# Last four heads' keys gathered by DMA from spare rows, and masks and normalisations on VectorE or GpSimd

## The chip, the cores and the metric

The kernel runs on one core of a Trainium2 chip. The metric is the device time of one execution in microseconds (us); the time before is the median of 3 runs. One execution was also recorded by the profiler. TensorE appears in the profile as PE (its weight loads as PEld), VectorE as DVE, ScalarE as ACT, GpSimd as POOL, and the queue of SyncE, which issues all DMAs here, as SP.

## What is computed

A transformer block on 2,048 tokens of width 448, in bf16: attention over a dilated local window, then a gated mixer over all tokens.

```python
def _A_ref(x, wqkv, wo):              # H = 16 heads of Dh = 28, W = 8, dil = 2
    q, k, v = split((x @ wqkv).reshape(B, S, 3, H, Dh))
    idx = pos[:, None] - arange(8) * 2         # each token sees 8 earlier ones, 2 apart
    logits = einsum('bhsd,bhswd->bhsw', q, k[idx]) * Dh ** -0.5   # masked where idx < 0
    return einsum('bhsw,bhswd->bhsd', softmax(logits), v[idx]) @ wo

def _B_ref(x, w_in, w_sp, b_sp, w_out):        # F = 1792, Fh = 896
    z = gelu(x @ w_in)
    z1, z2 = z[..., :Fh], layernorm(z[..., Fh:])
    g = einsum('ts,bsf->btf', w_sp, z2) + b_sp
    return (z1 * g) @ w_out

h = x + _A_ref(layernorm(x), wqkv, wo)
out = h + _B_ref(layernorm(h), w_in, w_sp, b_sp, w_out)
```

## The kernel before, in words

**The order of the work.** The kernel is written as some hundreds of jobs: a name, an engine, what it reads and writes, and an estimated duration. `Planner.order` (L272) plays them through with a model of the engines and PSUM's eight banks; among the jobs that are ready it takes the one with the lowest number in `PRIO` (L27), a hand-tuned rank per job. `LOOK` (L25) says how long an engine may be held for a job that isn't ready yet, `SWITCH` (L20) what a change of matmul kind is charged on TensorE, and `ON` (L67) puts single jobs on another engine than their first choice. The outcome is one fixed list of instructions per engine. On the chip each engine works through its list in that order and waits at an instruction until its semaphores are there, so an estimate that is wrong shows as a wait. A job of kind F is a full matmul of 128 rows, H a pair of 64-row ones, L a logit job.

**Layer norm and transposes.** The 16 tiles of 128 tokens get their statistics on VectorE (L696, L698), the root on GpSimd (L690, L691), and the normalisation `n0_m` on VectorE (L707). The first four tiles are transposed on TensorE, the others by DMA, for which a small copy `nd` (L575) widens the tile first. The result is `xhT`. After attention the same is done for h (`n1`, into `hnT`).

**Queries and keys.** The tokens go in six stretches `QT` (L80), t = 0 to 5: two of 128 tokens, one of 256, three of 512. In each, four groups g of four heads are made (L776): the weights in `wqk` give one head 32 of the 128 output rows, of which the last 4 are zero padding (`wpad`, L763), since a head has 28 dimensions. A group is a product `qk{t}_{g}` of six full matmuls (q and k, three blocks of 128 input rows each) and one pair of 64-row ones (L564). Its two PSUM banks are then copied by one job `qe{t}_{g}` into `qkT` (L581), rows g of q at index 2g and of k at 2g+1; the last 128 tokens also go to `qkL`. The weights reach `wqk` from `wraw` in the copies `wp` (L575).

**Attention.** 17 blocks b of up to 128 queries. For each, two logit jobs `lg{b}_0` and `lg{b}_1` (L874), eight matmuls of 28 rows each. The first takes the heads in rows 0 to 63 of all four groups, the second those in rows 64 to 127. Two exponentials follow on ScalarE (L883), the mask `mk{b}` over 16 heads in one VectorE multiplication (L889), 16 matmuls with V (`o{b}`, L898), the reciprocal and the scaling on VectorE (L906, L909), a copy `od`, a transpose by DMA into `OTs` and a copy `oc` into `OT` (L581). `project` makes the output projection `y` and the residual (L843).

**The mixer.** z2 for each of the 16 tiles: product (L564), GELU, statistics (L969), `n2_m` (L978) on VectorE. Eleven of the 16 products may run before the last exponential; they are copied raw and get their GELU later. z1 in 14 units (L1010). Then g = w_sp z2 in 28 chains of 16 matmuls (L1043), bias and product on VectorE (L1051, L1054), and the output matmuls (L1066), written out by SP. The weights w_sp arrive by transposing DMAs (`wsp_la`, `wsp_lb`, `wsp_hi`).

## Time and profile before

| | |
|---|---|
| median of 3 runs | 243.05 us (242.62 to 243.81) |
| the profiled execution | 243.6 us, of which 241.9 us from the first to the last instruction (the span) |
| granted TensorE clock | 1.000 |
| instructions | 4,239 |
| HBM read, written | 6.83 MB, 1.84 MB |

A page of the profile gives, for each engine, its busy time and share of the span, the same in 40 slices (tenths), and the chain that ended last, followed backwards from the last instruction. Its groups read: line, engine, operation, output <- input, shapes, count | busy us, mean ns of one | idle time before it and what ended it. The timeline has: start, duration, engine, line, operation, and in brackets the idle time before it. Matmuls are pipelined and their ends are modelled, so the cost of a sequence is read from the starts or from the chain of waits.

### The profile page before, as it was taken

The page shows a single profiled execution, that of the slowest core. Times are in us where ns is not written, and L with a number is a line of the kernel's source. Part 1 is how long each engine was busy: PE and PEld are TensorE (multiplying, and loading weights), DVE is VectorE, ACT ScalarE, POOL GpSimd, SP SyncE. Part 2 cuts the span into 40 slices and gives each one's busy share as a digit, 9 for nine tenths or more (in the row PEclk, how much of TensorE's full clock was granted, in tenths as well). Part 3 has the DMA queues.
Part 4 walks back from the last instruction along what each step waited for, and adds up shares of the span by engine and source line. Part 5 has one row for each costly group of instructions (what it writes and reads, how often), then busy time and mean ns, then how long its engine had stood idle before and what let it go on. Part 6 is the DMA issues. An engine that isn't in the chain of part 4 may idle for free.

```text
span 241.9 us, 4239 instructions
## 1 busy us (share of the span) xinstructions
PE 235.4 (97%) x1707; PEld 115.5 (48%) x1726; DVE 155.0 (64%) x319; ACT 92.6 (38%) x115; POOL 55.4 (23%) x110
## 2 busy tenths in 40 slices
PE   7999999999999999999999999999999999999995
PEld 5674545545545444444344444444444444434443
DVE  6999878998999999998573135106111920805554
ACT  2779777778989765666230000000000000033000
POOL 8535116255565533061111000000000000000000
PEclk9999999999999999999999999999999999999999
DMA  6954497958533999999899400000000020010112
GB/s 194 317 138 94 77 157 176 171 133 190 109 62 72 176 152 179 228 158 153 166 204 178 42 0 0 0 3 0 0 0 3 0 76 0 20 41 0 57 38 76
DMA packets 65923, 23.21 MB, mean 96 GB/s; under 512 B 58352, under 2 KB 65648, under 8 KB 65904
## 3 DMA queue, kind: packets, MB, share of 16 engines
q1 hardware_dynamic: 65904, 22.95, 46.9%
q8 instruction: 13, 0.21, 0.4%
q14 instruction: 6, 0.05, 0.1%
HBM read 6.83 MB, written 1.84 MB: 36 GB/s over the span
## 4 chain that ended last, share of the span: by engine, by line
PE 92%; DMA 2%; DVE 2%; SPq 1%; issue 1%; ACT 0%; ACTq 0%
PE psum L1043 40%; PE psum L564 37%; PE psum L1066 9%; PE psum L874 3%; PE psum L898 3%; DMA wraw<-in_A_wqkv_dram 2%; DVE E L889 1%; SPq L605 1%; DVE qkT L581 1%; ACT wqk L575 0%; PE psum L738 0%; DVE srg L1073 0%; PE psum L740 0%; ACTq L179 0%
## 5 line engine op out<-in xcount | busy, mean ns | idle before, releaser
L1051 DVE TENSOR_TENSOR ub<-psum,bb 128x512 bf16<-128x512 f32 x28 | 19.4, 691 | 50.4 <-PE psum L1043 50.0
L1043 PE MATMUL psum<-wsp_hi,z2p 128*128 128x512 bf16 x217 | 50.6, 379 | 0.4
L1010 ACT ACTIVATE z1p<-psum 128x1024 bf16<-128x1024 f32 x14 | 14.1, 1021 | 95.8 <-PE psum L564 95.8
L1043 PEld LDWEIGHTS psum<-wsp_hi,z2p 128*128 128x128 bf16 x224 | 21.8, 98 | 26.2 <-issue 0.4
L883 ACT ACTIVATE E<-psum 128x960 bf16<-128x960 f32 (+2 forms) x34 | 31.7, 973 | 6.5 <-PE psum L874 6.4
L564 PE MATMUL psum<-xhT,wqk 128*128 128x512 bf16 (+5 forms) x185 | 27.6, 306 | 1.0 <-issue 0.5
L1043 PE MATMUL psum<-wsp_la,z2p 128*128 128x512 bf16 x110 | 26.0, 379 | 0.1
L1043 PE MATMUL psum<-wsp_lb,z2p 128*128 128x512 bf16 x109 | 25.6, 379 | 0.2
L564 PE MATMUL psum<-w_in,hnT 128*128 128x448 bf16 (+1 forms) x128 | 24.3, 353 | 0.1
L564 PE MATMUL psum<-hnT,w_in 128*128 128x512 bf16 (+1 forms) x112 | 23.9, 379 | 0.0
L1066 PE MATMUL psum<-w_out,z1p 128*128 128x448 bf16 (+1 forms) x119 | 22.8, 341 | 0.0
L969 DVE BATCH_NORM_STATS2 st<-z2p 128x6 f32<-128x448 bf16 x32 | 19.2, 612 | 4.2 <-ACT z2p L965 3.7
L889 DVE TENSOR_TENSOR E<-E,maskb 128x1920 bf16<-128x1920 bf16 (+2 forms) x17 | 20.3, 1220 | 1.0 <-ACT E L883 1.0
L696 DVE BATCH_NORM_STATS2 st<-x_tm 128x6 f32<-128x448 bf16 x32 | 19.0, 612 | 1.5 <-DMA x_tm<-in_A_x_dram 1.3
L691 POOL TENSOR_TENSOR rs<-rs,negh 128x2 f32<-128x2 f32 (+2 forms) x22 | 18.6, 847 | 1.8
L564 PEld LDWEIGHTS psum<-xhT,wqk 128*128 128x128 bf16 (+1 forms) x192 | 12.6, 97 | 11.3 <-issue 3.2
L1043 PEld LDWEIGHTS psum<-wsp_la,z2p 128*128 128x128 bf16 x112 | 10.9, 98 | 13.3 <-issue 0.4
L1054 DVE TENSOR_TENSOR z1p<-ub,z1p 128x512 bf16<-128x512 bf16 x28 | 11.9, 424 | 8.4 <-ACT z1p L1010 7.5
L1043 PEld LDWEIGHTS psum<-wsp_lb,z2p 128*128 128x128 bf16 x112 | 11.0, 98 | 13.1
L581 ACT ACTIVATE qkT<-psum 128x1024 bf16<-128x1024 f32 (+2 forms) x22 | 15.0, 717 | 4.8 <-PE psum L564 4.5
L1066 PEld LDWEIGHTS psum<-w_out,z1p 128*128 128x128 bf16 x119 | 11.6, 98 | 10.3
L564 PEld LDWEIGHTS psum<-w_in,hnT 128*128 128x128 bf16 (+1 forms) x128 | 10.1, 97 | 12.7 <-issue 4.1
(63 smaller groups left out, 241.8 us busy)
## 6 DMA issues: line engine op xcount, KB each, us to landing
w_in<-in_B_w_in_dram SPq DMA_DIRECT2D x8, 224.0 KB, 3.2
out_dram<-srg SPq DMA_DIRECT2D x16, 112.0 KB, 1.7
x_tm<-in_A_x_dram SPq DMA_DIRECT2D x3, 448.0 KB, 6.2
w_out<-in_B_w_out_dram SPq DMA_DIRECT2D x1, 784.0 KB, 8.2
wraw<-in_A_wqkv_dram SPq DMA_DIRECT2D x1, 672.0 KB, 5.4
bb<-in_B_b_sp_dram SPq DMA_DIRECT2D x1, 512.0 KB, 6.4
wo<-in_A_wo_dram SPq DMA_DIRECT2D x1, 336.0 KB, 6.0
wv<-in_A_wqkv_dram SPq DMA_DIRECT2D x1, 336.0 KB, 6.2
```

Of the source, the lines that this page charges most:

```text
L564: ins = e.matmul(o, w, x, start=g not in seen, stop=left[g] == 0, **kw)
L581: return e.activation(o, i, AF.Copy) if eng == "act" else e.tensor_copy(o, i)
L691: (lambda e: e.tensor_tensor(R, A, negh[:, 0:1].to_broadcast([128, n]), ALU.pow), [rr, r_negh], r_rs[k][m:m + n])],
L696: [(lambda e: e.bn_stats(st[:, m, :], src), [rsrc], [r_st[k][m]])], dve_t(D))
L883: return e.activation(o, i, AF.Exp, scale=SCALE)
L889: return e.tensor_tensor(a, a, maskb[:, mi:mi + 1, pad:pad + nq].to_broadcast([NK, NHEAD, nq]), ALU.mult)
L969: [(lambda e, m=m, k=k: e.bn_stats(st3[:, m, k, :], z2p[:, m, D * k:D * (k + 1)]), [r_z2[m]], [r_st[2][m]])], dve_t(D))
L1010: return e.activation(o, i, AF.Gelu_apprx_tanh)
L1043: ins = e.matmul(psv(tk), z2p[:, s, 128 * fc:128 * fc + 128], w, start=(s == 0), stop=(s == NB - 1))
L1051: [(lambda e, tc=tc, s=s, tk=tk: e.tensor_tensor(ub[:, s, :], psv(tk), bb[:, 512 * tc:512 * tc + 512], ALU.add), [r_bb], [r_ub[s]])], dve_ ...
L1054: [(lambda e, fc=fc, tc=tc, s=s: e.tensor_tensor(z1p[:, fc, 512 * tc:512 * tc + 512], ub[:, s, :], z1p[:, fc, 512 * tc:512 * tc + 512], AL ...
L1066: ins = e.matmul(psv(tk, 0, c1 - c0), z1p[:, fc, 128 * m:128 * m + 128], w_out[:, fc, c0:c1], start=(fc == 0), stop=(fc == FC7 - 1))
```

## The change

In the three stretches of 512 tokens (t at least `T7` = 3) the fourth group makes only its queries (job `qs`, four matmuls one after the other, in one bank). The keys of its four heads, 28 dimensions each, are spread over the 4 padding rows per head of the seven other rows of groups (indices 0 to 6 of `wqk`, 7 x 4 = 28): four GpSimd copies `wr` put their weights there, after the products of t = 0, 1 and 2, which read the same weights, and ahead of those of t = 3. The usual copies out of PSUM carry them along into `qkT`. Four DMAs `qr{t}_{j}` per stretch, one per head, and four `qrL_{j}` at the end, each of which waits for all four `qe` copies of the stretch, gather the rows to index 7, and the logits of blocks in these stretches wait for them. The two logit jobs of a block become two kinds, L and M, and the planner's model of changes between them is another. Masks, `n0`, `n1` and `n2` may run on GpSimd, and `ON` puts there: six masks (blocks 1, 2, 5, 7, 8, 13), seven `n0`, six `n1`, nine `n2`. `ON` also moves some small copies between ScalarE, VectorE and GpSimd, and the ranks in `PRIO` are new.

```diff
@@ -17,58 +17,64 @@
 GEOM = [(r, 128, 0, 2) for r in range(2)] + [(256 + 240 * i + r, 120, 8, 2) for i in range(7) for r in range(2)] + [(1936, 112, 16, 1)]
 FC7 = 7
 NPT = 4
-SWITCH = {"FH": 0.096, "HF": 0.096, "FL": 0.1, "HL": 0.1, "LF": 0.03, "LH": 0.1}
+SWITCH = {"FH": 0.096, "HF": 0.096}
 FILL = 0.15
 TLAT = 0.9
 T0 = 0.8
 SAME = 0.0
-LOOK = {'pe': 1e-09, 'act': 0.1762690089245428, 'dve': 0.17500524126766434, 'pool': 0.04342214756282488, 'sp':
-        0.3037332826506372}
-PRIO = [0, 3, 4,
...
+LOOK = {'pe': 0.031998905655788515, 'act': 1e-09, 'dve': 0.1752115380099225, 'pool': 0.09185622963850922, 'sp':
+        0.5365358657565965}
+PRIO = [6, 3, 4, 5,
...
 KEY = dict(x=-10.145, xs=0.685, qk=-3.702, qkg=-1.064, v=-1.761, ve=-6.148, qe=-3.15, lg=-1.488, ex=5.497,
            mk=-3.215, o=2.696, om=0.603, oT=-1.054, hh=0.0, y=-5.759, h=0.564, ln2=4.478, hT=19.942, z2=74.834,
            z2s=0.028, zr=2.556, zrs=0.21, z1=34.42, z1s=2.041, g=84.462, gs=0.172, wo=1.509, wl=-9.273,
            wls=4.361, wp=-9.955)
 WINB = 2
-ON = {'xe0_0': 'dve', 'xe0_1': 'act', 'xe1_0': 'dve', 'nd0_9': 'dve', 'nd0_10': 'dve', 'wp0_0': 'act', 'wp0_1': 'act',
-      'wp1_0': 'act', 'wp4_0': 'act', 'wp4_1': 'act', 'qe4_1': 'dve', 'qe4_3': 'dve', 'oc1': 'pool', 've2': 'dve', 'od3':
-      'dve', 'oc3': 'pool', 've4': 'dve', 'od4': 'dve', 'oc5': 'pool', 'od6': 'dve', 'od7': 'dve', 'oc7': 'pool', 'nd1_5':
-      'dve', 've8': 'dve', 'oc9': 'pool', 've10': 'dve', 'oc11': 'pool', 'oc13': 'pool', 'nd1_10': 'dve', 'oc15': 'pool',
-      'nd1_14': 'dve', 'nd1_15': 'dve', 'z2c6': 'dve', 'z2c13': 'dve'}
+ON = {'n0_0': 'pool', 'xe0_1': 'act', 'n0_1': 'pool', 'n0_3': 'pool', 'n0_7': 'pool', 'nd0_8': 'dve', 'nd0_9': 'dve',
+      'n0_10': 'pool', 'nd0_11': 'dve', 'n0_12': 'pool', 'nd0_13': 'dve', 'n0_14': 'pool', 'nd0_14': 'dve', 'nd0_15': 'dve',
+      'wp2_0': 'act', 'wp3_0': 'act', 'wp3_1': 'act', 'qe0_2': 'dve', 'qe1_0': 'dve', 'qe3_1': 'dve', 'qe3_2': 'dve', 'qe5_0':
+      'dve', 'qe5_3': 'dve', 'od0': 'dve', 'mk1': 'pool', 'oc1': 'pool', 'nd1_0': 'dve', 've2': 'dve', 'mk2': 'pool', 'od2':
+      'dve', 'od3': 'dve', 'oc3': 'pool', 've4': 'dve', 'od4': 'dve', 'mk5': 'pool', 'oc5': 'pool', 'nd1_2': 'dve', 'n1_3':
+      'pool', 'nd1_3': 'dve', 'mk7': 'pool', 'oc7': 'pool', 'n1_4': 'pool', 'nd1_4': 'dve', 'n1_5': 'pool', 've8': 'dve',
+      'mk8': 'pool', 'oc9': 'pool', 'n1_7': 'pool', 'od11': 'dve', 'oc11': 'pool', 'n1_8': 'pool', 'n1_9': 'pool', 'nd1_9':
+      'dve', 'mk13': 'pool', 'oc13': 'pool', 'nd1_13': 'dve', 'nd1_14': 'dve', 'nd1_15': 'dve', 'n2_0': 'pool', 'n2_1':
+      'pool', 'n2_2': 'pool', 'n2_3': 'pool', 'n2_4': 'pool', 'n2_5': 'pool', 'z2c6': 'dve', 'n2_7': 'pool', 'n2_9': 'pool',
+      'n2_10': 'pool'}
 RAW2 = [0, 1, 2, 1, 1, 1, 1, 2, 1, 2, 1, 0, 0, 1, 0, 0]
 XEH = {0: 2}
 WLH = [4, 4, 8, 9, 18, 1, 4, 12, 24, 4, 14, 34, 6, 22, 21, 26]
@@ -77,6 +83,7 @@
 COLD = 6.4
 FIRST = [(0, 1), "q", (1, 2), (2, 4), "v", (4, 8), (8, 12), (12, 16), "o"]
 LN1G = [(0, 1), (1, 1), (2, 2), (4, 4), (8, 4), (12, 4)]
+T7 = 3
 QT = [(0, 128), (128, 256), (256, 512), (512, 1024), (1024, 1536), (1536, 2048)]
 
 BF16 = mybir.dt.bfloat16
@@ -339,11 +346,20 @@
             if j is self.filler and t < COLD:
                 dur *= 2
             if e == "pe":
-                if j.kind != pstate[0]:
-                    dur += SWITCH[pstate[0] + j.kind]
-                elif j.kind == "L" and t < te[e] + 0.05:
-                    dur -= 0.1
-                pstate[0] = j.kind
+                was, now = pstate[0], j.kind
+                if was.upper() in "LM" and now in "LM":
+                    if was.upper() != now and t < te[e] + 0.05:
+                        dur -= 0.1
+                        now = now.lower()
+                elif now in "LM":
+                    dur += 0.1
+                elif was in "LM":
+                    dur += 0.1
+                elif was in "lm":
+                    dur += 0.03
+                elif was != now:
+                    dur += SWITCH[was + now]
+                pstate[0] = now
             j.start = t
             j.end = t + dur
             te[e] = j.end
@@ -501,6 +517,8 @@
         r_V = [spot("V%d" % i, o_v + i * NHEAD * 64, NHEAD * 64) for i in range(NV)]
         r_OT = [[spot("OT%d_%d" % (i, k), o_ot, 4 * OTR * 2, gen=1) for k in range(2)] for i in range(OTR // 16)]
         r_OTs = [Res("OTs%d" % i) for i in range(2)]
+        r_qr = {t: [spot("qr%d_%d" % (t, j), o_qk, 8 * S_TOK * 2) for j in range(4)] for t in range(T7, len(QT))}
+        r_qrL = [Res("qrL%d" % j) for j in range(4)]
         r_xn = [Res("xn%d" % i) for i in range(NR)]
         r_xnd = [Res("xnd%d" % i) for i in range(NR)]
         r_otm = [Res("otm%d" % i) for i in range(NO)]
@@ -584,6 +602,13 @@
             eng = ON.get(name, eng)
             j = pl.job(name, eng, key, [(lambda e, f=f: f(e, eng), list(rr), list(ww)) for f, rr, ww in ops], durs[eng], use=use, rel=rel)
             j.alts = durs
+            return j
+
+        def either(name, key, ops, dve, gps):
+
+            eng = ON.get(name, "dve")
+            j = pl.job(name, eng, key, ops, {"dve": dve, "pool": gps}[eng])
+            j.alts = {"dve": dve, "pool": gps}
             return j
 
         def psk(tk, a, b):
@@ -703,9 +728,9 @@
             s = ringc[0] % NR
             ringc[0] += 1
             mu, rstd = mv[:, m, 0:1], rs[k][:, 1, m:m + 1]
-            pl.job("n%d_%d" % (k, m), "dve", key,
+            either("n%d_%d" % (k, m), key,
                    [(lambda e: e.tensor_scalar(xn[:, s, 0:D], src3[:, m, :], mu, rstd, ALU.subtract, ALU.mult),
-                     [rsrc, r_mv[k][m], r_rs[k][m]], [r_xn[s]])], dve_t(D, 4, 2))
+                     [rsrc, r_mv[k][m], r_rs[k][m]], [r_xn[s]])], dve_t(D, 4, 2), 0.85)
             if dup:
                 move("nd%d_%d" % (k, m), "pool", key, lambda: xn[:, s, D:512], lambda: xn[:, s, 384:D], [r_xn[s]], [r_xnd[s]],
                      {"pool": 0.34, "dve": 0.1})
@@ -760,7 +785,8 @@
 
         r_pad = [spot("wpad%d" % i, o_wp, 4 * 8 * 256) for i in range(8)]
         r_pad2 = [spot("wpad2_%d" % i, o_wp, 4 * 8 * 256) for i in range(2)]
-        pool("wpad", -57.5, [(lambda e: e.memset(wqk[:].rearrange("p c g (h d) -> p (c g h) d", h=4)[:, :, DH:32], 0.0), [], r_pad + r_pad2)], 0.4)
+        r_pad3 = [spot("wpad3_%d" % i, o_wp, 4 * 8 * 256) for i in range(4)]
+        pool("wpad", -57.5, [(lambda e: e.memset(wqk[:].rearrange("p c g (h d) -> p (c g h) d", h=4)[:, :, DH:32], 0.0), [], r_pad + r_pad2 + r_pad3)], 0.4)
         for g in range(4):
             for k in range(2):
                 move("wp%d_%d" % (g, k), "dve", KEY["wp"] + 0.3 * g,
@@ -775,7 +801,14 @@
 
         for t, (lo, hi) in enumerate(QT):
             n = hi - lo
-            for g in range(4):
+
+            for i in range(4 if t == T7 else 0):
+                pool("wr%d" % i, KEY["wp"] + 20.0 + i, [
+                    (lambda e, i=i: e.tensor_copy(
+                        wqk[:, :, 0:7, :].rearrange("p c g (j q) -> p c g j q", q=32)[:, :, :, :, DH + i],
+                        wraw[:, :, D + 336:2 * D].rearrange("p c (j q) -> p c j q", q=28)[:, :, :, 7 * i:7 * i + 7].rearrange(
+                            "p c j g -> p c g j")), W_qk, [r_pad3[i]])], 0.5)
+            for g in range(3 if t >= T7 else 4):
                 key = lo / 112.0 + KEY["qk"] + KEY["qkg"] * g
                 tk = Ticket(2)
 
@@ -785,13 +818,38 @@
                          for k in range(2) for c in range(3)],
                         [(k, psv(tk, k, n), wap(64 * k, 64, 3, 2 * g + k), xhT[64 * k:64 * k + 64, 3, lo:hi],
                           (64 * k, 0)) for k in range(2)])
-                product("qk%d_%d" % (t, g), key, f, r_pad[2 * g:2 * g + 2] + xh_res(lo, hi), n, 6, tk, hreads=r_pad2 + xh_res(lo, hi))
+                product("qk%d_%d" % (t, g), key, f, r_pad[2 * g:2 * g + 2] + r_pad3 + xh_res(lo, hi), n, 6, tk, hreads=r_pad2 + r_pad3 + xh_res(lo, hi))
                 qops = [(lambda e, eng, lo=lo, hi=hi, g=g, n=n, tk=tk: copy(e, eng, qkv(slice(2 * g, 2 * g + 2), lo, hi), psk(tk, 0, n).rearrange(
                     "p k (t r) -> p k r t", r=2)), [r_qk[t][g]])]
                 if hi == S_TOK:
                     qops.append((lambda e, eng, g=g, n=n, tk=tk: copy(e, eng, qkL[:, 2 * g:2 * g + 2, :], psk(tk, n - 128, n)), [r_qkL[g]]))
                 moves("qe%d_%d" % (t, g), "act", lo / 112.0 + KEY["qe"] + KEY["qkg"] * g, [(f, [], w) for f, w in qops],
                       {e: sum(evac_t(q)[e] for q in [2 * n, 256][:len(qops)]) for e in ("act", "dve")}, [tk], tk)
+            if t < T7:
+                continue
+            tk = Ticket(1)
+
+            def f(e, lo=lo, hi=hi, n=n, tk=tk):
+                for c in range(4):
+                    p = 128 if c < 3 else 64
+                    ins = e.matmul(psv(tk, 0, n), wap(0, p, c, 6), xhT[0:p, c, lo:hi], start=c == 0, stop=c == 3)
+                return ins
+            key = lo / 112.0 + KEY["qk"] + KEY["qkg"] * 3
+            pl.job("qs%d" % t, "pe", key, [(f, [r_pad[6]] + r_pad2 + r_pad3 + xh_res(lo, hi), [])], full_t(n, 4), acq=tk)
+            ps3 = (lambda tk=tk, n=n: psv(tk, 0, n))
+            qops = [(lambda e, eng, lo=lo, hi=hi, ps3=ps3: copy(e, eng, qkv(slice(6, 7), lo, hi)[:, 0], ps3().rearrange(
+                "p (t r) -> p r t", r=2)), [r_qk[t][3]])]
+            if hi == S_TOK:
+                qops.append((lambda e, eng, n=n, tk=tk: copy(e, eng, qkL[:, 6, :], psv(tk, 0, n)[:, n - 128:n]), [r_qkL[3]]))
+            moves("qe%d_3" % t, "act", lo / 112.0 + KEY["qe"] + KEY["qkg"] * 3, [(f, [], w) for f, w in qops],
+                  {e: sum(evac_t(q)[e] for q in [n, 128][:len(qops)]) for e in ("act", "dve")}, [tk], tk)
+            for j in range(4):
+                load("qr%d_%d" % (t, j), lambda j=j, lo=lo, hi=hi: qkv(slice(7, 8), lo, hi)[32 * j:32 * j + DH, 0],
+                     lambda j=j, lo=lo, hi=hi: qkT[32 * j + DH:32 * j + 32].rearrange("p g (r t) -> p (g r) t", r=2)[:, 0:14, lo // 2:hi // 2],
+                     [r_qr[t][j]], 0.6, (1.4, 0.2), key=lo / 112.0 + KEY["qe"] + 1.0, reads=r_qk[t])
+                if hi == S_TOK:
+                    load("qrL_%d" % j, lambda j=j: qkL[32 * j:32 * j + DH, 7, :], lambda j=j: qkL[32 * j + DH:32 * j + 32, 0:7, :],
+                         [r_qrL[j]], 0.6, (1.4, 0.2), key=lo / 112.0 + KEY["qe"] + 1.5, reads=r_qkL)
 
 
         o_jobs = {}
@@ -863,6 +921,11 @@
             for t, (lo, hi) in enumerate(QT):
                 if lo < t0 + sd * nq and hi > t0 - sd * pad:
                     rq += r_qk[t] if sd == 2 else r_qkL
+            rr = [[], []]
+            for t, (lo, hi) in enumerate(QT):
+                if t >= T7 and lo < t0 + sd * nq and hi > t0 - sd * pad:
+                    for j in range(2):
+                        rr[j] += (r_qr[t] if sd == 2 else r_qrL)[2 * j:2 * j + 2]
             for j in range(2):
                 tk = Ticket(2)
 
@@ -875,7 +938,7 @@
                                            src[p:p + DH, 2 * g, q0:q0 + nq], start=True, stop=True,
                                            tile_position=(p, 0))
                     return ins
-                lgs[(b, j)] = pl.job("lg%d_%d" % (b, j), "pe", b + KEY["lg"], [(f, rq, [])], 0.2, acq=tk, kind="L", after=[o_jobs.get(b - NE)])
+                lgs[(b, j)] = pl.job("lg%d_%d" % (b, j), "pe", b + KEY["lg"], [(f, rq + rr[j], [])], 0.2, acq=tk, kind="LM"[j], after=[o_jobs.get(b - NE)])
 
                 def f2(e, nq=nq, j=j, slot=slot, tk=tk):
                     o = E[:, slot, j * 8 * nq:(j + 1) * 8 * nq].rearrange("p (h q) -> p h q", q=nq)
@@ -887,7 +950,7 @@
             def fm(e, nq=nq, pad=pad, slot=slot, mi=sd - 1):
                 a = E[:, slot, 0:NHEAD * nq].rearrange("p (h q) -> p h q", q=nq)
                 return e.tensor_tensor(a, a, maskb[:, mi:mi + 1, pad:pad + nq].to_broadcast([NK, NHEAD, nq]), ALU.mult)
-            pl.job("mk%d" % b, "dve", b + KEY["mk"], [(fm, [r_mask[sd - 1]] + r_Eh[slot], [r_E[slot]])], dve_t(16 * nq, 2))
+            either("mk%d" % b, b + KEY["mk"], [(fm, [r_mask[sd - 1]] + r_Eh[slot], [r_E[slot]])], dve_t(16 * nq, 2) + 0.08, 2.6)
             tk = Ticket(1)
             vs = b % NV
 
@@ -974,10 +1037,10 @@
             if m % 2 == 1:
                 ln_rstd(2, m - 1, 2, mv3, KEY["z2"] + KEY["z2s"] * m)
                 for mm in (m - 1, m):
-                    pl.job("n2_%d" % mm, "dve", KEY["z2"] + KEY["z2s"] * mm,
+                    either("n2_%d" % mm, KEY["z2"] + KEY["z2s"] * mm,
                            [(lambda e, m=mm: e.tensor_scalar(z2p[:, m, :], z2p[:, m, :], mv3[:, m, 0:1], rs[2][:, 1, m:m + 1],
                                                             ALU.subtract, ALU.mult), [r_z2[mm], r_mv[2][mm], r_rs[2][mm]],
-                             [r_z2[mm]])], dve_t(FH, 4, 2))
+                             [r_z2[mm]])], dve_t(FH, 4, 2), 1.35)
 
 
         units = []
```

2 lines of the change are left out of this document (1 added, 1 removed), and 69 rows, old and new, of the table PRIO.

## The prediction

> **What bounds the kernel now.** I read the page first: the busy shares, then the 40 slices, then the chain that ended last.
>
> ```profile
> span 241.9 us, 4239 instructions
> PE 235.4 (97%) x1707; PEld 115.5 (48%) x1726; DVE 155.0 (64%) x319; ACT 92.6 (38%) x115; POOL 55.4 (23%) x110
> ...
> PE   7999999999999999999999999999999999999995
> ...
> DVE  6999878998999999998573135106111920805554
> ...
> POOL 8535116255565533061111000000000000000000
> ...
> PE psum L1043 40%; PE psum L564 37%; PE psum L1066 9%; PE psum L874 3%; PE psum L898 3%; DMA wraw<-in_A_wqkv_dram 2%; DVE E L889 1%; SPq L605 1%; DVE qkT L581 1%; ACT wqk L575 0%; PE psum L738 0%; DVE srg L1073 0%; PE psum L740 0%; ACTq L179 0%
> ```
>
> TensorE is full in every slice but the first and the last, and the chain is made of it. The view by windows gives the three stages (columns: window, its length, then busy us of PE, PEld, DVE, ACT, POOL, the clock, the DMA share, GB/s).
>
> ```profile
> 9.80:80.00 70.20, 68.77 (x867) 36.89 (x875) 64.42 (x128) 58.69 (x76) 31.86 (x51) 1.00 0.66 133
> 80.00:125.00 45.00, 44.90 (x247) 19.92 (x246) 38.89 (x92) 25.13 (x28) 13.78 (x29) 1.00 0.96 174
> 125.00:239.20 114.20, 113.67 (x542) 53.08 (x550) 44.33 (x80) 4.93 (x5) 1.82 (x4) 1.00 0.14 30
> ```
>
> The change acts in the first, attention, and a little in the second. There TensorE leaves 1.4 of 70.2 us free, but VectorE is busy for 92% of it as well. So matmul time removed there is worth its full length, if VectorE, GpSimd and the DMAs can follow. The two later stages shift as they are.
>
> **Part 1: three products shortened.** The chain of waits gives what matmuls cost in sequence (start, us, engine, line, count).
>
> ```profile
> 32.86 1.72 PE psum L564 x8
> ...
> 34.58 0.34 PE psum L874 x16
> ...
> 41.50 0.53 PE psum L874 x16
> ...
> 69.41 0.31 PE psum L874 x8
> 69.73 1.54 PE psum L564 x8
> ...
> 129.57 10.74 PE psum L1043 x49
> ```
>
> A q and k product of 512 tokens is the first row: six full matmuls and a 64-row pair, 1.72 us. One full matmul of 512 columns is 10.74 / 49 = 0.219 us. The new `qs` has four in a row, 0.88 us. That is 0.84 us less, in three stretches: **-2.5 us**. If its last one, of 64 rows, still costs a change as the pair did (the product is 1.72 - 6 x 0.219 = 0.41 us for the pair, against one 0.219), the gain is down by at most 0.19 each: -1.9. I take -2.5, as the planner of the kernel before charges no change without a tile position.
>
> **Part 2: order of the logits.** 16 logit matmuls take 0.34 us in some places and 0.53 in others, and eight alone 0.31. The new model of kinds favours an L right next to an M. I count in the timeline (logits at 16.0 to 73.3 us) seven pairs at about 0.34, six at 0.53 and eight single jobs. If all became short pairs, the gain would be 6 x 0.19 + 4 x (0.62 - 0.34) = 2.3 us; if none did, 0, and worse order could lose as much. The new ranks have other things to serve as well; I take under half: **-1.0 us**.
>
> **Part 3: weights and gather.** The four `wr` copies stand between the last product of t = 2 and the first of t = 3. Nearest row: GpSimd's copies of 64 elements, below, 0.355 us; each moves 112 scattered elements, so 0.4 to 0.6, four make about 2 us on GpSimd. TensorE meanwhile has value products, logits and o of the first blocks. Cover gone, it would be 2 us once; I take **+0.3 us**.
>
> The gather is 12 DMAs of 28 KB and four small ones; no DMA of before copies few rows to few rows. The bounds come from the issues that land soonest and latest (us to landing last in the row).
>
> ```profile
> out_dram<-srg SPq DMA_DIRECT2D x16, 112.0 KB, 1.7
> ...
> xhT<-xn SPq DMA_TRANSPOSE x12, 2.5
> ...
> wsp_la<-in_B_w_sp_dram SPq DMA_TRANSPOSE x8, 4.6
> OTs<-otm SPq DMA_TRANSPOSE x8, 3.2
> ```
>
> So 1.7 to 4.6 us; I take 2.5, the row that also goes from SBUF to SBUF at that time. The plan charges 0.6 for the issue and 1.6 to land, so 0.3 us more than it allows for. Four gathers (three stretches and `qrL`) at 0.3: **+1.2 us**. Does TensorE wait there at all? In the kernel before, the first logits that need t = 3 came right behind its last copy:
>
> ```profile
> 30.86 1.02 ACT L581 ACTIVATE qkT<-psum 128x1024 bf16<-128x1024 f32 x1 [0.59 <-PE psum L564]
> 32.88 0.97 ACT L883 ACTIVATE E<-psum 128x960 bf16<-128x960 f32 x1 [0.99 <-PE psum L874]
> ...
> 28.52 0.58 SPq L605 DMA_DIRECT2D w_in<-in_B_w_in_dram  x1
> 29.20 1.21 SPq L604 DMA_TRANSPOSE xhT<-xn  x1
> 30.45 1.30 SPq L604 DMA_TRANSPOSE wsp_la<-in_B_w_sp_dram  x1
> ```
>
> The copy ends at 31.88 and ScalarE was idle for 0.99 us until the logits came. So this is a place without slack in the attention chain; TensorE itself has the products of t = 4 to run, if the list puts them ahead. Queued behind the waiting logit job are those products, `o` and values, for which VectorE and ScalarE wait. On SP a gather waits for the last of four copies, and behind it stand transposes of `xhT`, `OTs` and `wsp_la`; the 16 issues cost about 16 x 0.58 = 9 us of SP. `wsp_la` isn't read before 113 us, and `xhT` of the last tiles not before t = 5, so I cost that at nothing; cover gone, it is one issue group of four, 2.3 us.
>
> At the start `ON` moves the two widest weight copies from ScalarE to VectorE:
>
> ```profile
> 7.57 1.29 DVE L575 COPY wqk<-wraw 128x336 bf16<-128x336 bf16 x5 [0.28 <-DMA wraw<-in_A_wqkv_dram]
> ...
> 9.80 0.34 PE L564 MATMUL psum<-xhT,wqk 64*128 64x128 bf16 x6 [0.19 <-ACT wqk L575]
> ```
>
> The 64-row matmuls waited for ScalarE; VectorE's five copies before took 0.26 each. It can bring 0.3 us or, queued behind more copies, cost as much: 0.
>
> **Part 4: masks and normalisations to GpSimd.** Rows by form (busy us, mean ns):
>
> ```profile
> L889 DVE TENSOR_TENSOR E<-E,maskb 128x1920 bf16<-128x1920 bf16 x14 | 16.9, 1230 | 0.3 <-ACT E L883 0.3
> L707 DVE TENSOR_SCALAR xn<-x_tm,mv,rs 128x448 bf16<-128x448 bf16 x32 | 12.4, 412 | 1.2 <-POOL rs L691 1.1
> ...
> L575 POOL COPY xn<-xn 128x64 bf16<-128x64 bf16 x22 | 7.5, 355 | 9.2 <-DVE xn L707 9.2
> ...
> L575 DVE CAST V<-psum 128x896 bf16<-128x896 f32 x4 | 4.4, 1092 | 1.5 <-PE psum L564 1.5
> ...
> L581 DVE CAST qkT<-psum 128x1024 bf16<-128x1024 f32 x2 | 2.4, 1224 | 1.0 <-PE psum L564 1.0
> ...
> L575 DVE COPY xn<-xn 128x64 bf16<-128x64 bf16 x6 | 1.1, 185 | 0.1
> ...
> L575 DVE CAST xhT<-psum 128x256 bf16<-128x256 f32 x1 | 0.4, 424 | 0.2 <-PE psum L740 0.2
> ```
>
> VectorE in the first stage: six masks leave (7.4 us), eight of the thirteen normalisations (3.3), two `qe` copies of t = 4 (2.4) and one of values (1.1); there come two `qe` copies of t = 3 (2.4), those of t = 0, 1 and 5 (0.42 for 256 columns, 1.22 for 1,024, 0.7 between for 512: about 3.5) and eight small `nd` and `od` copies (1.5). Net -6.8: 57.6 us in a stage of 66.7 (70.2 - 3.5), 86%. No gain in time by itself, since TensorE ends the stage; what it buys is room for waits. The nine `n2` help VectorE in the second stage, where nothing waits for it long.
>
> GpSimd: no such multiplication is in the trace. The nearest rows are its copies, in the timeline, alone and beside a mask:
>
> ```profile
> 36.43 3.31 DVE L889 TENSOR_TENSOR E<-E,maskb 128x1920 bf16<-128x1920 bf16 x2
> 36.59 2.20 POOL L581 COPY OT<-OTs 128x1024 bf16<-128x1024 bf16 x1 [3.25 <-DMA OTs<-otm]
> ...
> 69.21 1.26 POOL L581 COPY OT<-OTs 128x960 bf16<-128x960 bf16 x1 [0.32 <-DMA OTs<-otm]
> 69.26 1.34 DVE L707 TENSOR_SCALAR xn<-x_tm,mv,rs 128x448 bf16<-128x448 bf16 x1
> ...
> 80.66 1.27 POOL L581 COPY OT<-OTs 128x960 bf16<-128x960 bf16 x1 [1.10 <-DMA OTs<-otm]
> ...
> 87.96 0.24 POOL L575 COPY xn<-xn 128x64 bf16<-128x64 bf16 x1 [2.31 <-DVE xn L707]
> ```
>
> 960 elements in 1.27 us and 64 in 0.24 are 1.15 ns an element: 1,920 in 2.3 us if the second input is free, 4.6 if it costs as much as the first. I take 2.6, near the copy row, which is also what the change's plan charges. A normalisation by the same slope is 0.7 to 1.2; 0.85. GpSimd's first stage: 31.9 + 6 x 2.6 + 8 x 0.85 + 2.0 - 8 x 0.355 = 53.5 of 66.7 us. It holds, but these operations get in each other's way: at 69.26 the normalisation takes 1.34 us, not 0.41, and ends 0.13 us after the copy; at 36.43 two masks take 3.31, not 2.5, and the copy 2.20. So what runs on GpSimd has to be added to VectorE's eleven remaining masks (13.5 us): 67.0 us, against the 66.7 that TensorE needs plus two raw z2 products that it could bring forward (the row at 69.73 is one, 1.54 us): 69.8. Just covered: **0**. ScalarE, 58.7 us of 70.2, loses and gains copies of about the same sum; TensorE covers it.
>
> The Trainium skill ("SBUF — State Buffer", Who interferes with whom) says that a VectorE instruction with two SBUF inputs, or in a fast two-port mode, and a GpSimd one that reads SBUF exclude each other whole; the rows at 36.43 and 69.26 agree.
>
> **Sum.** -2.5 - 1.0 + 0.3 + 1.2 = **-2.0 us**. The profiled execution took 243.6 us, 0.55 above the median, so 241.6 for such a one and **241.0** for the median; with Part 2 between -1.7 and -0.5 and the gather between 0.9 and 1.5, 240.0 to 241.9.
>
> **The rivals.** *GpSimd becomes the bound (slower).* With m us per mask the two engines' shared work is 37.9 + 6m + 13.5 us. Above 69.8, so from m = 3.1, TensorE is idle for the rest; from m = 3.6 that idle time exceeds the 3.2 us that Parts 1 to 3 save without the gather. At m = 4.0 it is 75.4 - 69.8 = 5.6 us, net +2.4: 245.4. For it: masks that collided, and 92% VectorE already. Against: GpSimd's 31.9 us holds blocked time already, so some is counted twice. Chance 0.21.
>
> The Trainium skill ("GPSIMD Engine Reference", Performance versus the Vector engine) speaks against this move: two-input operations at half VectorE's rate, 4,497 ns for 2,048 fp32. Scaled to 1,920 that is an estimate of 4.2 us a mask, by which the formula gives about 246.6; no row of before shows it.
>
> *The gather eats it (no change).* If the DMAs land like `OTs`, 3.2 us, that is 1.0 over the plan; in three stretches 3.0, with -3.2 leaves 242.8. For it: no slack at 31.88 us, and DMA engines that are full in the windows at that time (1.10, below); against: TensorE has other products. Chance 0.20.
>
> ```profile
> 40.00:48.00 8.00, 7.84 (x104) 4.12 (x102) 7.06 (x12) 5.37 (x7) 2.54 (x3) 1.00 1.10 191
> ```
>
> *All of it.* Every logit pair short and no new wait: -2.5 - 2.3, 238.2. Chance 0.13.
>
> **How the numbers follow.** The forecast has 0.44, and 0.02 are for mishaps of other kinds. About 0.5% (1.2 us) is what a measurement of this kernel can tell from no change, so faster is below 241.8 and slower above 244.3. Faster: 0.40 of the forecast, 0.13, and 0.03 of the gather: 0.56. Slower: 0.17 of GpSimd's case and 0.01: 0.18. Within: 0.26. The range takes in the forecast, the gather, the upper part of the full gain and GpSimd's case up to m = 4: 238.8 to 245.4.
>
> **What would show it.** Part 1: the products at `qs` at 0.88 us, three times. Part 2: few rows of 0.53 among the logits. Part 3: idle time of TensorE just ahead of logits of blocks from 4 on, released by a DMA. Part 4: the mean of the GpSimd mask (2.6 or 4), VectorE's masks and normalisations not longer than 1.23 and 0.41. Wrong would be the whole, if the first window with z1 matmuls and without logits came later than at 80 us although VectorE has less to do.

## The result and the profile after

The changed kernel takes **276.26 us** (median of 6 runs, 275.53 to 278.85) against 243.12 us for the kernel before (6 runs): a ratio of 1.1378, 95% interval 1.1317 to 1.1439. The forecast was 241.0, the range ended at 245.4. The profiled execution took 276.29 us. Its page (span, busy times, slices of PE and POOL, granted clock, chain):

```profile
span 274.6 us, 4265 instructions
...
PE 246.7 (90%) x1716; PEld 116.5 (42%) x1716; DVE 159.2 (58%) x304; ACT 93.1 (34%) x114; POOL 124.2 (45%) x132
...
PE   6888989769975999599729999999999999999996
...
POOL 7899893947496999599489300000000000000000
PEclk9999999968996899889986999999999999999999
...
PE 54%; POOL 19%; DVE 19%; DMA 4%; issue 3%; SPq 0%; ACT 0%; POOLq 0%
```

TensorE is no longer full: the slices from 20 to 150 us have holes. The chain now runs over GpSimd and VectorE for 38% of the span; by engine it was, before:

```profile
PE 92%; DMA 2%; DVE 2%; SPq 1%; issue 1%; ACT 0%; ACTq 0%
```

The span grew by 32.7 us. TensorE's idle time (span less busy) went from 241.9 - 235.4 = 6.5 to 274.6 - 246.7 = 27.9 us, +21.4. The other 11.3 is that TensorE is *longer busy* with less work: the mean granted clock fell from 1.000 to 0.956, and 4.4% of 274.6 us is 12.1 us. The stages, after (columns as in the prediction: length, busy PE, PEld, DVE, ACT, POOL, clock, DMA share, GB/s), then the last of them before:

```profile
9.80:80.00 70.20, 62.11 (x744) 32.02 (x745) 62.01 (x106) 48.31 (x65) 53.84 (x57) 0.95 0.65 119
80.00:125.00 45.00, 37.81 (x268) 16.62 (x268) 35.12 (x73) 25.97 (x28) 38.14 (x40) 0.89 0.62 114
125.00:160.00 35.00, 27.82 (x125) 11.25 (x124) 15.93 (x38) 12.60 (x15) 23.97 (x18) 0.90 0.73 143
```

```profile
125.00:160.00 35.00, 34.84 (x160) 15.85 (x162) 11.88 (x22) 0.95 (x1) 1.82 (x4) 1.00 0.31 51
```

All three stages lose, also the two that the prediction let "shift as they are"; GpSimd is busy in all of them. The groups of the moved operations (count | busy, mean ns):

```profile
L1041 POOL TENSOR_SCALAR z2p<-z2p,mv,rs 128x896 bf16<-128x896 bf16 x9 | 30.6, 3408 | 0.2
...
L732 POOL TENSOR_SCALAR xn<-x_tm,mv,rs 128x448 bf16<-128x448 bf16 x13 | 25.2, 1939 | 0.4
L952 POOL TENSOR_TENSOR E<-E,maskb 128x1920 bf16<-128x1920 bf16 (+1 forms) x6 | 23.1, 3863 | 1.3 <-ACT E L946 1.3
...
L952 DVE TENSOR_TENSOR E<-E,maskb 128x1920 bf16<-128x1920 bf16 (+2 forms) x11 | 18.4, 1681 | 0.1
...
L732 DVE TENSOR_SCALAR xn<-x_tm,mv,rs 128x448 bf16<-128x448 bf16 x19 | 12.6, 679 | 8.9 <-POOL rs L716 8.2
```

On GpSimd a mask takes 3.9 us, the normalisation of 448 elements 1.9, that of 896 elements 3.4. What stayed on VectorE got longer in the mean as well (masks 1,220 to 1,681 ns, norms 412 to 679), because of a few that took up to 3.9 us. One place in the timeline shows how this reaches TensorE (start, duration; in brackets the idle time before), and the windows of 2 us behind it what follows:

```profile
51.67 3.81 POOL L952 TENSOR_TENSOR E<-E,maskb 128x1920 bf16<-128x1920 bf16 x1
...
52.73 3.77 DVE L952 TENSOR_TENSOR E<-E,maskb 128x1920 bf16<-128x1920 bf16 x1
...
56.56 0.56 PE L961 MATMUL psum<-V,E 128*128 128x29 bf16 x16 [2.12 <-DVE E L952]
```

```profile
54.00:56.00 2.00, 0.44 (x14) 0.24 (x10) 2.00 (x1) 1.55 (x2) 1.49 (x1) 1.00 1.16 297
56.00:58.00 2.00, 0.94 (x24) 0.68 (x24) 2.00 (x4) 0.46 (x1) 0.00 (x0) 0.81 0.22 83
58.00:60.00 2.00, 1.98 (x13) 0.81 (x14) 1.58 (x5) 1.48 (x2) 1.06 (x3) 0.50 0.00 0
60.00:62.00 2.00, 2.00 (x18) 0.90 (x17) 1.83 (x1) 0.14 (x1) 2.00 (x2) 0.50 0.87 158
62.00:64.00 2.00, 2.00 (x22) 1.04 (x19) 2.00 (x2) 2.00 (x3) 1.93 (x1) 0.50 0.25 88
```

GpSimd starts a mask at 51.67. VectorE's own mask, 1.1 us at most other places, starts at 52.73 and ends 1.0 us after GpSimd's: it was held up until that one had ended. TensorE, which has `o` next, is busy for 1.4 of the 4 us from 54 to 58. Then its clock is at 0.50 for some 7 us. So one late mask cost 2.6 us of idle time and over 3 us of half-speed work. Holes with half clock behind them also stand at 81 to 91, 112 to 119 and 139 to 149 us. At 81 us VectorE is held behind a GpSimd mask again; at 112 us it is late after 4.3 us of waiting for normalisations on GpSimd, and at 139 us g waits for `n2`.

### The profile page after: what moved, and what is told of

It reads as the page before. It is cut to its first block, busy times and chain, and to the rows that moved or that the text cites. A ratio compares the mean times of both kernels' runs of the same rounds, so it can differ in the third digit from the quotient of the medians.

```text
span 274.6 us, 4265 instructions
## 1 busy us (share of the span) xinstructions
PE 246.7 (90%) x1716; PEld 116.5 (42%) x1716; DVE 159.2 (58%) x304; ACT 93.1 (34%) x114; POOL 124.2 (45%) x132
## 4 chain that ended last, share of the span: by engine, by line
PE 54%; POOL 19%; DVE 19%; DMA 4%; issue 3%; SPq 0%; ACT 0%; POOLq 0%
PE psum L1106 35%; PE psum L582 9%; PE psum L1129 8%; POOL z2p L1041 7%; DVE st L1032 3%; POOL rs L716 3%; DVE xn L732 3%; POOL xn L732 3%; DVE E L952 3%; POOL E L952 3%; DMA wraw<-in_A_wqkv_dram 3%; DVE xn L593 2%; DVE st L721 1%; DVE otm L972 1%; DMA OTs<-otm 1%
## 5 line engine op out<-in xcount | busy, mean ns | idle before, releaser
L1106 PE MATMUL psum<-wsp_lb,z2p 128*128 128x512 bf16 x112 | 28.0, 388 | 6.9 <-issue 5.5
L1041 POOL TENSOR_SCALAR z2p<-z2p,mv,rs 128x896 bf16<-128x896 bf16 x9 | 30.6, 3408 | 0.2
L1106 PE MATMUL psum<-wsp_la,z2p 128*128 128x512 bf16 x112 | 28.5, 397 | 0.3 <-DVE mv L1035 0.3
L582 PE MATMUL psum<-w_in,hnT 128*128 128x448 bf16 (+1 forms) x128 | 26.6, 379 | 0.1
L582 PE MATMUL psum<-xhT,wqk 128*128 128x512 bf16 (+5 forms) x168 | 24.8, 310 | 1.9 <-DVE wqk L593 0.9
L732 POOL TENSOR_SCALAR xn<-x_tm,mv,rs 128x448 bf16<-128x448 bf16 x13 | 25.2, 1939 | 0.4
L952 POOL TENSOR_TENSOR E<-E,maskb 128x1920 bf16<-128x1920 bf16 (+1 forms) x6 | 23.1, 3863 | 1.3 <-ACT E L946 1.3
L952 DVE TENSOR_TENSOR E<-E,maskb 128x1920 bf16<-128x1920 bf16 (+2 forms) x11 | 18.4, 1681 | 0.1
L1136 DVE TENSOR_TENSOR srg<-psum,x_tm 128x448 bf16<-128x448 f32 (+1 forms) x17 | 9.7, 592 | 14.7 <-PE psum L1129 14.7
L732 DVE TENSOR_SCALAR xn<-x_tm,mv,rs 128x448 bf16<-128x448 bf16 x19 | 12.6, 679 | 8.9 <-POOL rs L716 8.2
L1106 PEld LDWEIGHTS psum<-wsp_la,z2p 128*128 128x128 bf16 x112 | 11.3, 101 | 15.0 <-issue 2.2
```

The source lines that it names most:

```text
L582: ins = e.matmul(o, w, x, start=g not in seen, stop=left[g] == 0, **kw)
L732: [(lambda e: e.tensor_scalar(xn[:, s, 0:D], src3[:, m, :], mu, rstd, ALU.subtract, ALU.mult), [rsrc, r_mv[k][m], r_rs[k][m]], [r_xn[s]])] ...
L952: return e.tensor_tensor(a, a, maskb[:, mi:mi + 1, pad:pad + nq].to_broadcast([NK, NHEAD, nq]), ALU.mult)
L1041: [(lambda e, m=mm: e.tensor_scalar(z2p[:, m, :], z2p[:, m, :], mv3[:, m, 0:1], rs[2][:, 1, m:m + 1], ALU.subtract, ALU.mult), [r_z2[mm], ...
L1106: ins = e.matmul(psv(tk), z2p[:, s, 128 * fc:128 * fc + 128], w, start=(s == 0), stop=(s == NB - 1))
```

## The experiments

In what follows, a charge is the duration that the planner puts down for a job. The theory after this trace: the length of GpSimd's operations is the loss. Its rival: the gather, or the new order itself.

**Shortened GpSimd operations.** The order on every engine stays that of the changed kernel; only instructions on GpSimd get shorter: masks over 11 heads, normalisations as copies.

```diff
-a = E[:, slot, 0:NHEAD * nq]        # mk on pool
+a = E[:, slot, 0:11 * nq]
-e.tensor_scalar(z2p[:, m, :], z2p[:, m, :], mv3.., rs.., subtract, mult)   # n2 on pool; n0, n1 alike
+e.tensor_copy(z2p[:, m, :], z2p[:, m, :])
```

All 28 of them:

> The changed kernel with the same instructions in the same order on every engine, but the 28 GpSimd masks and normalisations shortened to about what the plan charges for them: a mask covers 11 of 16 heads (by its rate in the changed kernel 2.6 us instead of 3.8), each n0, n1 and n2 on GpSimd is a plain copy (by the copy rows about 0.7 and 1.2 us instead of 1.9 and 3.4). Left out: part of the masking, and the normalisation of those tiles. Theory GpSimd (the length of these operations is the loss): 240 to 246 us. Rival gather (TensorE waits for the key DMAs): stays above 260, with idle TensorE ahead of logits released by DMA. Rival order (the new ranks are bad by themselves): stays above 260 without such waits.

Measured 254.43 us (ratio 1.0434, 1.0246 to 1.0621). With 2.70 us a mask, 0.56 and 0.94 us for the copies, about the planner's charges or below, 21.8 of the 33 us are gone, and 11 are not. That is neither what the theory expected (246 us or less) nor what its rivals did (260 or more). Then each kind alone, in one execution each:

> Only the six GpSimd masks shortened, to 11 of 16 heads (the rest of the mask is left out); 7 us less on GpSimd. Theory GpSimd: 266 to 270 us, by the share of 7 in the 42 us that all three take off. Rivals gather and order: 274 to 277.

> Only the 13 normalisations n0 and n1 on GpSimd shortened to copies (the normalisation of these tiles is left out); 15.5 us less on GpSimd. Theory GpSimd: 261 to 266 us. Rivals gather and order: 274 to 277.

> Only the nine n2 on GpSimd shortened to copies (the normalisation of these tiles is left out); 19 us less on GpSimd, in the stage from 98 to 150 us of the changed kernel. Theory GpSimd: 257 to 264 us. Rivals gather and order: 274 to 277.

The masks alone give 267.85 (-8.4) and `n2` alone **260.73 (-15.5)**, both as the theory expected. `n0` and `n1` alone give 275.5 (-0.8), a miss, and no more than the executions of the changed kernel differ among themselves. The largest part is the one that the prediction left without a price. Where it was lost: in the changed kernel,

```profile
122.75 10.02 POOL L1041 TENSOR_SCALAR z2p<-z2p,mv,rs 128x896 bf16<-128x896 bf16 x3
...
140.20 6.95 POOL L1041 TENSOR_SCALAR z2p<-z2p,mv,rs 128x896 bf16<-128x896 bf16 x2
...
143.91 1.86 PE L1106 MATMUL psum<-wsp_lb,z2p 128*128 128x512 bf16 x4 [5.45 <-issue]
```

and with `n2` short:

```profile
80.00:125.00 45.00, 40.69 (x296) 18.50 (x296) 39.01 (x83) 31.20 (x34) 32.31 (x44) 0.92 0.71 144
125.00:160.00 35.00, 35.00 (x170) 15.73 (x168) 15.27 (x33) 7.38 (x9) 7.64 (x13) 1.00 0.75 132
```

The first chains of g read z2p tile by tile, and five norms in two rows on GpSimd take 17 us. Inside these chains TensorE stands idle for 5.45 us. (The profile writes "issue"; but the first norm of the pair that ends at 147.15 ends at about 143.7, 0.2 us ahead of the matmul.) With `n2` short, the stage from 125 to 160 us is full again.

**Everything back on VectorE.** `ON` without the 28 entries, all else as changed, ranks too:

> The changed kernel with all 28 masks and normalisations back on VectorE; gather, ranks and the rest as changed. Theory GpSimd: the 33 us go but for what the order loses, since the ranks were made for other lengths: 242 to 254 us. Rival gather: above 260, with TensorE idle ahead of logits released by DMA.

262.21 us (1.0792, 1.0761 to 1.0823): 14 us better than the change, and 19 worse than before. A miss: no long GpSimd operation is left, and the loss isn't gone. **The logits not waiting for the gather**, on top of the shortened kernel:

> The kernel with all 28 GpSimd operations shortened (254.4 us), same order on every engine, but the logits do not wait for the gather: for the last group of the late stretches they read index 5 in place of 7 (left out: the right keys of four heads there); the DMAs still run. Rival gather: the rest of 11 us against before comes from these waits, so 245 us or less. Otherwise: 253 to 256, no change.

256.39 us (1.0552, 1.0519 to 1.0585), no gain. There the wait for the gather isn't what holds.

**GpSimd's operations by themselves**: the kernel *before* with 21 extra instructions on GpSimd from 130 us on, on tiles that nobody reads any more.

> The kernel before with 21 extra GpSimd operations on dead tiles from about 130 us on, where GpSimd is idle and VectorE is busy for 30%: three each of the mask's multiplication (1,920 elements), the same with a plain second input, a copy of 1,920, the normalisation of 448 and of 896 elements, the normalisation of 448 with constants in place of per-row scalars, a copy of 448. Time 243 to 245 us. Theory: their length is their own, so the shortest of each is 3.8 (mask), 1.85 (448) and 3.35 us (896) here too. Rival: VectorE holds them up in the changed kernel, and here they take what the plan charges, 2.6, 0.85 and 1.35 us. Open: whether the constants make the normalisation as short as a copy.

251.07 us (1.0333, 1.0303 to 1.0363), a miss in time: work that nobody waits for cost 8 us. The timeline and the waits of TensorE (line, releaser: us, times, longest):

```profile
130.16 11.64 POOL L1088 TENSOR_TENSOR xn<-xn,maskb 128x1920 bf16<-128x1920 bf16 x3
...
153.67 5.71 POOL L1090 COPY xn<-otm 128x1920 bf16<-128x1920 bf16 x3
159.49 5.83 POOL L1091 TENSOR_SCALAR xn<-otm,mv,rs 128x448 bf16<-128x448 bf16 x3
165.42 10.26 POOL L1092 TENSOR_SCALAR xn<-otm,mv,rs 128x896 bf16<-128x896 bf16 x3
...
130.30 7.84 DVE L979 TENSOR_SCALAR z2p<-z2p,mv,rs 128x896 bf16<-128x896 bf16 x2 [1.21 <-POOL rs L692]
...
143.16 2.81 DVE L1055 TENSOR_TENSOR z1p<-ub,z1p 128x512 bf16<-128x512 bf16 x1
...
154.72 1.09 DVE L1055 TENSOR_TENSOR z1p<-ub,z1p 128x512 bf16<-128x512 bf16 x1
...
173.38 0.43 DVE L1055 TENSOR_TENSOR z1p<-ub,z1p 128x512 bf16<-128x512 bf16 x1
```

```profile
PE psum L1044 <- DVE z2p L979: 5.4, 1, 5.4
```

The lengths are GpSimd's own, as the theory expected, with VectorE idle or not (medians of single ones): 3.83 us a mask, 1.86 a norm of 448, 3.35 of 896, while a copy of 1,920 takes 1.86. Two normalisations on VectorE, 0.51 us each where nothing is beside them, ended at 138.14, right behind the second mask on GpSimd (130.16 + 2/3 of 11.64 = 137.9). TensorE waited 5.4 us for them, and its clock was at 0.50 from 138 to 141.

**What are the other 11 to 19 us?** Four kernels with ranks, and the engines of the small copies, found anew by the same search over the planner's model, of the same length for each:

```diff
 # g_dve: gather kept, all on VectorE     n_dve: T7 = 6 (no gather), all on VectorE
 # a_true: engines as changed, measured charges     g_free: the same, engines free
-... dve_t(D, 4, 2), 0.85)
+... dve_t(D, 4, 2), 1.87)
-... dve_t(16 * nq, 2) + 0.08, 2.6)
+... dve_t(16 * nq, 2) + 0.08, 3.82)
-... dve_t(FH, 4, 2), 1.35)
+... dve_t(FH, 4, 2), 3.35)
```

> Gather and new q/k products kept; all masks and normalisations on VectorE as in the kernel before; the ranks found anew for just this mixture, by a search of about 25 minutes from the kernel before's ranks. If the loss is due to the GpSimd operations and to an order made for other lengths, the gather alone is near neutral: 240 to 247 us, clock 0.99 or more, PE waits on the gathered group under 3 us. If the gather itself (its landing of 3 to 4 us ahead of the logits) costs the 19 us that the run with everything back on VectorE still lost, then 253 us or more here too.

> Control for the run with the gather and re-found ranks: the same code without the gather (all heads' k by matmul), everything on VectorE, ranks from the same search of the same length. Both theories: 240 to 246 us. What the gather is worth by itself is the difference of the two: by the sum of the prediction's Parts 1 to 3, -2 us; if the gather costs much, +8 or more.

> The changed kernel with every operation on the engine that it has there (all 28 on GpSimd), but with the planner's prices for them replaced by the measured ones (mask 2.6 to 3.82, norm 0.85 to 1.87, z2p norm 1.35 to 3.35) and the ranks found anew. If the loss is an order made for wrong prices, and slow operations can be covered once the order knows their length: 246 to 252 us and PE idle under 12 us. If the operations cost by themselves, because they are latency on the chain and hold VectorE up beside them, 256 to 266 us.

> Gather kept, measured prices in the planner, and the search free to put each mask and normalisation on either engine (it left 4 masks, 6 of the xn norms and 7 of the z2p norms on GpSimd). If knowing the length is enough, the best of all: 240 to 245 us. If GpSimd operations hold VectorE up in ways that no price covers, slower than the same with everything on VectorE by 3 us or more.

| | us | ratio (95%) | clock in the profile |
|---|---|---|---|
| gather, all on VectorE | 261.52 | 1.0721 (1.0674 to 1.0767) | 0.974 |
| no gather, all on VectorE | 248.47 | 1.0205 (1.0180 to 1.0231) | 1.000 |
| gather, 28 on GpSimd, right charges | 264.12 | 1.0858 (1.0825 to 1.0890) | 0.974 |
| gather, engines free | 262.98 | 1.0777 (1.0677 to 1.0876) | 0.974 |

With the measured charges and an order made for them the kernel with the same 28 operations is 12.1 us faster (264.1 against 276.3). It stays the slowest of the four, but each of them is a single order, and orders of one kind turn out below to lie up to 9 us apart, so the three with the gather cannot be ranked. Between them and the one without it the gather seemed to cost 13 us. Its waits in the kernel with all on VectorE:

```profile
PE psum L928 <- DMA qkT<-qkT: 7.3, 5, 2.5
```

In the chain of waits of this run and the one with everything back on VectorE, a gather lands 2.9 to 4.9 us after its issue begins; the planner charges 2.2 (0.6 for the issue, 1.6 to land). New theory: the order counts on too early a landing. Three runs: the landing charged at 3.4 instead of 1.6; the order of the 261.5 us run without the wait; and the gather put into the order of the kernel before.

```diff
-[r_qr[t][j]], 0.6, (1.4, 0.2), ...      # g_land
+[r_qr[t][j]], 0.6, (3.2, 0.2), ...
-src[p:p + DH, 2 * g + 1, ...]           # g_dve_nowait: g = 3 reads index 5
+src[p:p + DH, (2 * g + 1 if g < 3 else 5), ...]
```

> Gather kept, everything on VectorE, but the planner charges 3.4 us (measured) instead of 1.6 us from the end of a gather's issue to its landing; ranks found anew in the same way. If the 13 us between the runs with and without the gather come from an order that counts on too early a landing: 246 to 252 us, within 4 us of the run without the gather (248.5), PE waits on the gathered group under 2 us and no clock under 0.9. If the gather costs by itself (queue, bandwidth, latency of the logits), 256 us or more.

> The run with the gather and re-found ranks (261.5 us) with the same order on every engine, the gathers still issued, but the logits of the last four heads reading another, finished group, so that nothing waits for a gather (scores of these heads are those of other heads). If the wait for the landing is the cost: 248 to 253 us, and the stretch at a clock of 0.66 (40 to 50 us) gone. If the gather's traffic or its issues on SP are the cost: 258 us or more.

> Parts 1 to 3 put into the kernel before with as little else as can be: its engines, its ranks (those of the fourth q/k group go to its half product, each gather follows its evacuation), no search. If only the waits for the landings cost: 3 to 5 gathers that PE must wait 1 to 3 us for, 247 to 256 us. If ranks made for another job list cost by themselves, 258 us or more. Both: not under 243.

251.90 (1.0328, 1.0280 to 1.0377), 258.69 (1.0613, 1.0557 to 1.0669) and 261.85 us (1.0739, 1.0692 to 1.0786). The first speaks for the theory, the second against it: without any wait 2.8 us come back, not 10. The third fell where its expectation puts ranks that were made for another list of jobs (258 or more). So each kind got a second order, from another seed:

> A second, independent order for the run with the measured landing charged (251.9 us), from a search with another seed. If the charge for the landing is the cause of the 9.6 us between the two gather runs: again 249 to 256 us, and below its partner with the short charge. If 251.9 was a lucky order: 258 to 263 us, like the other five orders with the gather.

> A second order with the gather at the short charge, everything on VectorE (the first: 261.5 us). If the charge is the cause: 258 to 264 us again. If orders scatter by 10 us whatever is charged: anywhere from 249 to 264, and no gap to its partner.

> A second order without the gather, everything on VectorE (the first: 248.5 us). If re-finding the ranks costs some 5 us by itself, since the planner's charges are not the chip's: 246 to 251 us. If the first was an unlucky order: 241 to 244 us, the time of the kernel before.

251.60 (1.0334, 1.0275 to 1.0393), **252.31** (1.0370, 1.0313 to 1.0427) and 245.99 us (1.0091, 1.0064 to 1.0118). The second order with the short charge is as good as those with the long one: **the theory of the charge falls**. Two orders of one search, for one list of jobs and charges, lie 9 us apart (261.5 and 252.3). What holds over all orders found: without the gather 246.0 and 248.5, with it 251.6, 251.9, 252.3, 261.5 and, in the ranks of the kernel before, 261.9. From best to best the gather is 1.0328 / 1.0091 = 1.023, some 5.7 us, and at the closest pair 1.0328 / 1.0205 = 1.012, 3 us. In none does it gain. The place, in the second order with the short charge:

```profile
35.30 1.83 ACT L937 ACTIVATE E<-psum 128x960 bf16<-128x960 f32 x2 [5.42 <-PE psum L928]
...
30.50 3.25 SPq L621 DMA_DIRECT2D qkT<-qkT  x4
...
34.88 0.59 PE L928 MATMUL psum<-qkT 28*128 28x120 bf16 x16 [1.16 <-DMA qkT<-qkT]
...
37.03 0.83 PE L928 MATMUL psum<-qkT 28*128 28x120 bf16 x32 [1.23 <-DMA qkT<-qkT]
```

```profile
38.00:40.00 2.00, 1.52 (x5) 0.68 (x6) 1.16 (x1) 2.00 (x3) 0.00 (x0) 0.65 1.87 137
40.00:42.00 2.00, 2.00 (x22) 0.71 (x21) 1.25 (x2) 1.64 (x3) 0.15 (x1) 0.50 0.63 132
```

The last copy of t = 3 on ScalarE ends at 29.89; then ScalarE has nothing for 5.42 us. Before, the same gap was 0.99 us. The four issues take 3.25 us of SP's queue one behind the other, the last two heads land 3.3 us after it, and TensorE runs dry and goes to half clock. Both orders without the gather have a mean clock of 1.000; in the profile of every order with it the clock drops (means of 0.973 to 0.993). But the wait isn't the whole price: in the profile of the 251.9 us order, with the longer charge, no wait of TensorE is put down to a gather, and it is no faster.

What stays open is how the gather's 3 to 6 us split into the wait, SP's queue and the luck of few orders. That the queue has a part is only argued, from the run without the wait, whose longest wait is for a load that SP issues too:

```profile
PE psum L573 <- DMA w_in<-in_B_w_in_dram: 3.0, 1, 3.0
```

Nor was it measured what the changed kernel's own ranks, made for other lengths, add. The three best orders with the gather and nothing moved to GpSimd are 8.0 to 9.1 us over the kernel before, near the 11 us that were left after the shortening. No version found beats the kernel before.

## Why the prediction was wrong

**What bounds, Part 1: right, a little less.** The short product runs as

```profile
40.13 0.98 PE psum L835 x4
```

against 0.88 forecast and 1.72 for the pair of before: 3 x 0.74 = 2.2 us, not 2.5. It could not show in the total, as TensorE had 21 us more of idle time elsewhere.

**Part 4, "a normalisation by the same slope is 0.7 to 1.2; 0.85" and "I take 2.6": the step that failed.** The mask's bounds (2.3 to 4.6) held 3.81; the value taken lay at the wrong end, and the estimate beside the GpSimd rival from the Trainium skill ("GPSIMD Engine Reference", Performance versus the Vector engine), 4.2 us, was nearer. The norm's bounds did not hold: 1.86. The slope of a copy, 1.15 ns an element, did not carry over to an operation that subtracts and multiplies: 3.7 to 4.1. `n2` got no price at all, and took 3.35. "Where nothing waits for it long" was true of a kernel in which it takes 0.51 us; here its length was worth 15.5. So the terms that failed are "Just covered: **0**" for the masks and normalisations and the missing one for `n2`: shortening all 28 gave back 21.8 us.

**The sum on two engines.** With the measured 3.81 and 1.86 the rival's formula gives 37.9 + 22.9 + 13.5 + 8 x 1.01 = 82.4 us against 69.8, so 12.6 us idle and, less 3.2 saved, about 252.5 us. The rival named the right engine and the collisions, and its price stopped at m = 4 for masks alone. It would still have missed more than half, for three reasons. It filled up the sum of two engines, while in the first window after the change neither is full (62.0 and 53.8 of 70.2 us), and TensorE waits for single late operations. The second stage wasn't in it. And a wait was priced at its length: here 21.4 us of new idle time brought 11.3 us of slower matmuls.

**Part 3, "+1.2": mis-sized, and in the wrong unit.** Landing was taken at 2.5 us, 0.3 over the plan each; it is 2.9 to 4.9. What counts is copy to logits, 5.0 and 7.1 us in the rows above (34.88 and 37.03 less 29.89): four issues in one queue and then the landing. "Idle time of TensorE just ahead of logits, released by a DMA" was the sign named, and it is there in most runs with the gather and without GpSimd's long operations. In the profile of the changed kernel no wait of TensorE is put down to a gather: something else came later each time. Instead of -2.0 us Parts 1 to 3 are +3 to +6, by the orders found.

**The start, "0".** The first q and k products, after and before:

```profile
10.37 0.51 PE L582 MATMUL psum<-xhT,wqk 128*128 128x128 bf16 x6 [0.94 <-DVE wqk L593]
```

```profile
8.22 1.28 PE L564 MATMUL psum<-xhT,wqk 128*128 128x128 bf16 x18
```

They come 2.15 us later. The prediction looked at the copies that `ON` moves, not at the ranks of the loads, which now issue 784 KB of x ahead of the weights `wraw`, against 448 before; the largest load of `wraw` lands 7.4 us after its issue, against 5.4.

**Part 2 and the ranks.** The order was forecast to gain 1.0. In the timeline of the changed kernel seven pairs of logit jobs run short, as before, three run long, three jobs stand in one row and eleven alone; at the prices of the kernel before that is 7.9 us against 8.0. Two orders found anew for the jobs of before cost 2.7 and 5.2 us by themselves: what is better by the planner's charges need not be better on the chip, and that was not among the rivals.

**The range** ended at 245.4, since each case was one mechanism in the first stage. They came together, in two stages. The sign that the prediction named for being wrong as a whole is there: the last logits run at 95 us.

## What to carry to other kernels

Before an operation moves to another engine, take its duration there from a row with the same operation, not the same number of elements; without one, plan by the upper bound, for every operation that moves. Where a fixed order is laid out by charges, ask what waits for the operation whose charge is wrong: shortening nine `n2` by 21.8 us in all gained 15.5, six masks by 6.8 us gained 8.4, thirteen norms by 17 us nearly nothing. And where the matmul engine is full, price a hole of 2 to 5 us at its length plus 1.7 or 3.4 us for the slow clock after it.
